# Recurrence and maxout MLP on one core: fixed issue order, short first blocks, most inputs transposed by DMA through DRAM, four tokens per partition in the stores

## The chip, the cores and the metric

The kernel runs on one core of a Trainium2 chip. The metric is device time in microseconds (us), as the median of a few executions. "Span" is the time from the first to the last instruction in one profiled execution; it is about 2 us shorter than the time of the same execution. TensorE is PE in the profile (PEld its weight loads), VectorE is DVE, ScalarE is ACT, GpSimd is POOL, SyncE is SP.

## The reference

```python
# x, f_logit: (4, 6144, 256); lower_bound: (256,); w1, w2: (256, 1024); w_out: (1024, 256); float32
f = lb + (1 - lb) * sigmoid(f_logit)
h = f[:, t] * h + (1 - f[:, t]) * x[:, t]        # for every t; y[:, t] = h
g = maximum(y @ w1, y @ w2)
out = g @ w_out                                  # (24576, 256)
```

Both kernels use max(y w1, y w2) = relu(y (w2 - w1)) + y w1. So the first layer needs one product with wd, the scaled difference of w2 and w1, and the second layer sums y (w1 w_out), whose matrix w13 is computed once, and relu(...) w_out. The features lie on the 128 partitions, because the recurrence is a scan along the tokens of each feature. f and x lie in memory with tokens as rows, so they have to be transposed.

## The kernel before

Tokens go in blocks of TB = 512. Inputs come in chunks of 1,024 tokens by a GpSimd DMA that casts to BF16, and TensorE transposes them in 128x128 pieces:

```python
def turn(j, slot):                       # 2 of the 16 transposes of a block
    c, o = home[j]
    s, q = divmod(slot, FC // 2)
    if q == 0:
        turned[j, s] = ps_t.tile([P, KC, TB], BF16, name=("fT", "xT")[s])
    dst = turned[j, s]
    for h in range(KC):
        nc.tensor.transpose(dst[:, h, q * P : (q + 1) * P],
            ins[c][s][:, o * NSB + q, h * P : (h + 1) * P], ident_b[:])
# [...]
# project(): the second layer; 128 consecutive tokens are the stationary tile
tok = slice(i * P, (i + 1) * P)
steps = [(y[:, kc, tok], w13[:, kc, :]) for kc in range(KC)]
steps += [(rts[j, fc][:, tok], wob[:, fc, :]) for fc in range(FC)]
# [...] stores of 256 tokens, rows of 1 KB
nc.sync.dma_start(out=out[r0 : r0 + 2 * P, :].rearrange("(r p) d -> p r d", p=P), in_=osb[:])
# [...] main loop: only TensorE's order is set by hand
with tc.manual_schedule(engines={ENG.PE}):
    for j in range(NBLK + 1):
        # [...] load(c) four blocks ahead
        for fc in range(FC):
            if j < NBLK: hidden(j, fc)            # first layer, 2 matmuls of 512 columns, relu on ACT
            if j > 0: project(j - 1, fc)          # 5 matmuls of 256 columns
            if j + 2 < NBLK: turn(j + 2, fc)      # 2 transposes
        if j + 2 < NBLK: recurrence(j + 2)        # sigmoid on ACT; v, ff and two scans on DVE
```

One pass of the inner loop is called a slot below; eight slots are a block.

Of the kernel before, what the change touches and what calls it, by code (L numbers as in the profile page):

```python
# [8 lines left out]
FP32 = mybir.dt.float32  # L9
# [4 lines left out]
P = 128  # L14
# [3 lines left out]
def kernel(  # L18
# [18 lines left out]
    NSB = TB // P  # L37
    CH = 2 * TB
    assert S % CH == 0
    NBB = S // TB  # L40
    NBLK = B * NBB
    chunks = [(0, 1), (1, 1)] + [(j, 2) for j in range(2, NBLK, 2)]
    home = {j + o: (c, o) for c, (j, n) in enumerate(chunks) for o in range(n)}
# [3 lines left out]
    inpool = ctx.enter_context(tc.tile_pool(name="inp", bufs=4))  # L47
# [5 lines left out]
        tc.tile_pool(name="ps_t", bufs=1, space=bass.MemoryType.PSUM)  # L53
# [7 lines left out]

    ident_f = const.tile([P, P], FP32)
    make_identity(nc, ident_f[:])
    ident_b = const.tile([P, P], BF16)
    nc.vector.tensor_copy(out=ident_b[:], in_=ident_f[:])  # L65

    om = const.tile([P, KC], FP32)
    nom = const.tile([P, KC], FP32)
    lbc = const.tile([P, KC], FP32)
    nc.sync.dma_start(out=lbc[:], in_=lower_bound.rearrange("(h p) -> p h", p=P))  # L70
# [5 lines left out]
    ins = {}  # L76

    def load(c):
        j, n = chunks[c]
        b, k = divmod(j, NBB)  # L80
        t0, nt = k * TB, n * TB
        ni = nt // P
        tiles = []
        for name, src in (("fn", f_logit), ("xn", x)):
            nat = inpool.tile([P, CH // P, D], BF16, name=name)
            nc.gpsimd.dma_start(  # L86
                out=nat[:, 0:ni, :],
                in_=src[b, t0 : t0 + nt, :].rearrange("(i p) d -> p i d", p=P),
            )
            tiles.append(nat)  # L90
        ins[c] = tiles

    ys = {}
    turned = {}

    def turn(j, slot):
        c, o = home[j]
        s, q = divmod(slot, FC // 2)
        if q == 0:
            turned[j, s] = ps_t.tile([P, KC, TB], BF16, name=("fT", "xT")[s])  # L100
        dst = turned[j, s]
        for h in range(KC):
            nc.tensor.transpose(  # L103
                dst[:, h, q * P : (q + 1) * P],
                ins[c][s][:, o * NSB + q, h * P : (h + 1) * P],
                ident_b[:],
            )

    def recurrence(j):
        fT, xT = turned[j, 0], turned[j, 1]  # L110
        prev = ys.get(j - 1) if j % NBB else None
        u = midpool.tile([P, KC, TB], BF16, name="u")
        nc.scalar.activation(out=u[:], in_=fT[:], func=AF.Sigmoid, scale=-1.0)  # L113
        v = midpool.tile([P, KC, TB], BF16, name="v")
        nc.vector.tensor_tensor(out=v[:], in0=u[:], in1=xT[:], op=ALU.mult)  # L115
        ff = midpool.tile([P, KC, TB], BF16, name="ff")
        y = ypool.tile([P, KC, TB], BF16, name="y")
        for h in range(KC):
            nc.vector.tensor_scalar(  # L119
                out=ff[:, h, :],  # L120
                in0=u[:, h, :],
                scalar1=nom[:, h : h + 1],
                scalar2=1.0,
                op0=ALU.mult,
                op1=ALU.add,
            )
            nc.vector.tensor_tensor_scan(  # L127
                out=y[:, h, :],
                data0=ff[:, h, :],
                data1=v[:, h, :],  # L130
                initial=0.0 if prev is None else prev[:, h, TB - 1 : TB],
                op0=ALU.mult,
                op1=ALU.add,
            )
        ys[j] = y

    def weight_prep():
        w1n = wpool.tile([P, KC, DFF], FP32)
        w2n = wpool.tile([P, KC, DFF], FP32)
        wob = wpool.tile([P, FC, D], BF16)  # L140
        w1b = wpool.tile([P, KC, DFF], BF16)
        wdf = wpool.tile([P, KC, DFF], FP32)
        wd = wpool.tile([P, KC, DFF], BF16)
        for g in range(2):
            cols = slice(g * DFF // 2, (g + 1) * DFF // 2)
            for w, src in ((w1n, moe_w1), (w2n, moe_w2)):
                nc.scalar.dma_start(
                    out=w[:, :, cols],
                    in_=src[:, cols].rearrange("(kc p) f -> p kc f", p=P),
                )  # L150
        nc.gpsimd.dma_start(
            out=wob[:], in_=moe_w_out.rearrange("(fc p) c -> p fc c", p=P)
        )
        for g in range(2):
            cols = slice(g * DFF // 2, (g + 1) * DFF // 2)
            nc.scalar.copy(out=w1b[:, :, cols], in_=w1n[:, :, cols])  # L156
            nc.vector.tensor_tensor(  # L157
                out=wdf[:, :, cols],
                in0=w2n[:, :, cols],
                in1=w1n[:, :, cols],  # L160
                op=ALU.subtract,
            )
            for kc in range(KC):
                nc.vector.tensor_scalar_mul(
                    out=wd[:, kc, cols], in0=wdf[:, kc, cols], scalar1=om[:, kc : kc + 1]
                )
        w1T = wpool.tile([P, FC, D], BF16)
        for kc in range(KC):
            for g in range(FC // 4):
                pt = ps_d.tile([P, TB], BF16, name="dT")  # L170
                for q in range(4):
                    fc = 4 * g + q
                    nc.tensor.transpose(
                        pt[:, q * P : (q + 1) * P],
                        w1b[:, kc, fc * P : (fc + 1) * P],
                        ident_b[:],
                    )
                nc.scalar.copy(
                    out=w1T[:, 4 * g : 4 * g + 4, kc * P : (kc + 1) * P],
                    in_=pt[:].rearrange("p (q d) -> p q d", q=4),  # L180
                )
        w13 = wpool.tile([P, KC, D], BF16)
        for kc in range(KC):
            psw = ps_o.tile([P, 2, D], FP32, name="psO")
            for fc in range(FC):
                nc.tensor.matmul(  # L186
                    psw[:, 0, :],
                    lhsT=w1T[:, fc, kc * P : (kc + 1) * P],
                    rhs=wob[:, fc, :],
                    start=(fc == 0),  # L190
                    stop=(fc == FC - 1),
                )
            nc.scalar.mul(w13[:, kc, :], psw[:, 0, :], om[:, kc : kc + 1])
        return wd, wob, w13
# [3 lines left out]
    def hidden(j, fc):  # L198
        y = ys[j]
        dT = ps_d.tile([P, TB], FP32, name="dT")  # L200
        for kc in range(KC):
            nc.tensor.matmul(  # L202
                dT[:],
                lhsT=wd[:, kc, fc * P : (fc + 1) * P],
                rhs=y[:, kc, :],
                start=(kc == 0),
                stop=(kc == KC - 1),
            )
        rt = rpool.tile([P, TB], BF16, name="rt")
        nc.scalar.activation(out=rt[:], in_=dT[:], func=AF.Relu)  # L210
        rts[j, fc] = rt

    pos = {}

    def project(j, slot):
        i, half = divmod(slot, 2)
        g, r = divmod(i, 2)
        y = ys[j]
        if r == 0 and half == 0:
            pos[j] = ps_o.tile([P, 2, D], FP32, name="psO")  # L220
        ps = pos[j]
        tok = slice(i * P, (i + 1) * P)
        steps = [(y[:, kc, tok], w13[:, kc, :]) for kc in range(KC)]
        steps += [(rts[j, fc][:, tok], wob[:, fc, :]) for fc in range(FC)]
        n = len(steps)
        for s in range(half * n // 2, (half + 1) * n // 2):
            nc.tensor.matmul(  # L227
                ps[:, r, :],
                lhsT=steps[s][0],
                rhs=steps[s][1],  # L230
                start=(r == 0 and s == 0),
                stop=(r == 1 and s == n - 1),
                skip_group_check=True,
            )
        if r == 1 and half == 1:
            osb = opool.tile([P, 2, D], FP32, name="osb")
            nc.vector.tensor_copy(out=osb[:], in_=ps[:])  # L237
            r0 = j * TB + 2 * g * P
            nc.sync.dma_start(
                out=out[r0 : r0 + 2 * P, :].rearrange("(r p) d -> p r d", p=P),  # L240
                in_=osb[:],
            )

    started = {c: chunks[c][0] for c in range(len(chunks))}
    ahead = 4
    for c in range(len(chunks)):
        if started[c] < ahead:
            load(c)
    for slot in range(FC):
        turn(0, slot)  # L250
    recurrence(0)
    wd, wob, w13 = weight_prep()
    for slot in range(FC):
        turn(1, slot)
    recurrence(1)
    with tc.manual_schedule(engines={ENG.PE}):
        for j in range(NBLK + 1):
            for c in range(len(chunks)):
                if started[c] == j + ahead:
                    load(c)  # L260
            for fc in range(FC):
                if j < NBLK:
                    hidden(j, fc)
                if j > 0:
# [35 lines left out]
```

## Time and profile before

| | before |
|---|---|
| time, median | 445.1 us |
| span of the profiled execution | 443.3 us |
| TensorE busy | 423.0 us, 95% |
| slot with transposes / without | 1.09 us / 0.98 us |
| main loop runs freely from | 25.2 us |
| last matmul ends to end of span | 4 us |

From the page of the kernel before: busy time and instructions of each engine; then two DMA queues (packets, megabytes, share of the time of 16 DMA engines; q0 is GpSimd's, q1 that of SP); then the chain that ended last, by engine.

```profile
PE 423.0 (95%) x3488; PEld 309.8 (70%) x3488; DVE 247.0 (56%) x345; ACT 278.5 (63%) x442; POOL 44.9 (10%) x57
...
q0 software_dynamic: 50992, 25.69, 46.1%
q1 hardware_dynamic: 26384, 25.17, 18.4%
...
PE 94%; DMA 4%; POOL 1%; DVE 0%; issue 0%; POOLq 0%
```

TensorE binds. What a transpose costs it is read from the timeline (start in us, duration, engine, line, instruction, count), in the steady part and in the last block, where nothing is left to transpose.

```profile
206.59 0.28 PE L103 MATMUL xT<-ident_b,xn 128*128 128x128 bf16 x2
206.71 0.59 PE L202 MATMUL dT<-y,wd 128*128 128x512 bf16 x2
207.14 0.71 PE L227 MATMUL psO<-wob,rt 128*128 128x256 bf16 x5
207.68 0.28 PE L103 MATMUL xT<-ident_b,xn 128*128 128x128 bf16 x2
...
428.87 0.59 PE L202 MATMUL dT<-y,wd 128*128 128x512 bf16 x2
429.30 0.38 PE L227 MATMUL psO<-w_182,y 128*128 128x256 bf16 x2
429.52 0.49 PE L227 MATMUL psO<-wob,rt 128*128 128x256 bf16 x3
429.85 0.59 PE L202 MATMUL dT<-y,wd 128*128 128x512 bf16 x2
```

Matmuls overlap, so starts are to be compared, not durations. The two transposes start at 206.59 us and the next matmul at 206.71: about 0.06 us each. The slot is 207.68 - 206.59 = 1.09 us, and 429.85 - 428.87 = 0.98 us without transposes, so by the slots a transpose costs 0.11 / 2 = 0.055 us. All 768 of them are 768 x 0.055 = 42 us.

The start, in the timeline of TensorE (in brackets the idle time before and what ended it):

```profile
13.38 1.01 PE L103 MATMUL fT<-ident_b,fn 128*128 128x128 bf16 x8 [13.38 <-DVE ident_b L65]
...
18.02 0.39 PE L202 MATMUL dT<-y,wd 128*128 128x512 bf16 x1 [0.34 <-DVE y L127]
...
23.51 1.91 PE L186 MATMUL psO<-wob,w1T 128*128 128x256 bf16 x16 [1.83 <-DMA wob<-in_moe_w_out_dram]
```

### The profile page before, as it was taken

Reading aid. Unit: us, or ns where it says so; the run is one execution under the profiler, and the core shown is the slowest. Engines: PE = TensorE matmul, PEld = TensorE weight load, DVE = VectorE, ACT = ScalarE, POOL = GpSimd, SP = SyncE. Lnnn points to the kernel's source line nnn. Section 1 sums busy time; section 2 is a strip of 40 time slices with the busy share of each in tenths; the row PEclk is TensorE's granted clock in tenths of the full one; section 3 lists DMA queues with packets and bytes.
Section 4 is the critical chain, followed back from the end, with each engine's and each line's share of the span. In section 5 each row is a group of like instructions: output and inputs, shape, how many; then the busy total and the mean of one; then the engine's idle time right before and its main releaser. Section 6 shows DMA issues by size and latency. Waiting matters only on the chain.

```text
span 443.3 us, 8434 instructions
## 1 busy us (share of the span) xinstructions
PE 423.0 (95%) x3488; PEld 309.8 (70%) x3488; DVE 247.0 (56%) x345; ACT 278.5 (63%) x442; POOL 44.9 (10%) x57
## 2 busy tenths in 40 slices
PE   0689999999999999999999999999999999999996
PEld 0567777777777777777777777777777777777765
DVE  2744665565556546655655565466546655654631
ACT  3666666666666766666666666666766666666661
POOL 6300101001001001010010010010100100000000
PEclk9999999999999999999999999999999999999999
DMA  8999769487487495694874965956948731212112
GB/s 221 198 198 215 138 124 152 83 146 123 94 140 127 91 163 94 123 151 87 146 119 99 140 121 96 163 95 124 149 85 149 120 95 48 72 49 71 57 64 95
DMA packets 78501, 53.49 MB, mean 121 GB/s; under 512 B 2688, under 2 KB 77440, under 8 KB 78464
## 3 DMA queue, kind: packets, MB, share of 16 engines
q0 software_dynamic: 50992, 25.69, 46.1%
q1 hardware_dynamic: 26384, 25.17, 18.4%
q10 hardware_dynamic: 1088, 2.10, 1.5%
q8 instruction: 27, 0.44, 0.4%
q14 instruction: 10, 0.08, 0.1%
HBM read 53.48 MB, written 25.17 MB: 177 GB/s over the span
## 4 chain that ended last, share of the span: by engine, by line
PE 94%; DMA 4%; POOL 1%; DVE 0%; issue 0%; POOLq 0%
PE psO L227 47%; PE dT L202 37%; PE xT L103 5%; PE fT L103 5%; DMA wob<-in_moe_w_out_dram 4%; POOL fn L86 1%; POOL xn L86 1%; PE psO L186 0%; DVE osb L237 0%; POOL ident_f masks.py:199 0%; POOL ident_f masks.py:197 0%; POOLq masks.py:199 0%; POOLq L284 0%
## 5 line engine op out<-in xcount | busy, mean ns | idle before, releaser
L210 ACT ACTIVATE rt<-dT 128x512 bf16<-128x512 f32 x384 | 226.8, 597 | 142.2 <-PE dT L202 142.1
L227 PE MATMUL psO<-wob,rt 128*128 128x256 bf16 x1536 | 229.8, 273 | 0.0
L202 PE MATMUL dT<-y,wd 128*128 128x512 bf16 x768 | 228.2, 379 | 1.1 <-DVE y L127 1.1
L227 PEld LDWEIGHTS <-rt 128*128 128x128 bf16 x1536 | 150.3, 98 | 57.5
L237 DVE COPY osb<-psO 128x512 f32<-128x512 f32 x96 | 66.4, 692 | 152.5 <-PE psO L227 152.5
L127 DVE TENSOR_TENSOR_SCAN y<-ff,y,v 128x512 bf16<-128x512 bf16 x88 | 108.2, 1272 | 1.5
L227 PE MATMUL psO<-w_182,y 128*128 128x256 bf16 x384 | 73.3, 273 | 0.0
L227 PEld LDWEIGHTS <-y 128*128 128x128 bf16 x384 | 37.6, 98 | 44.4
L103 PE MATMUL fT<-ident_b,fn 128*128 128x128 bf16 x384 | 52.2, 221 | 13.4 <-DVE ident_b L65 13.4
L202 PEld LDWEIGHTS <-wd 128*128 128x128 bf16 x768 | 59.6, 98 | 0.9 <-DVE y L127 0.5
L103 PE MATMUL xT<-ident_b,xn 128*128 128x128 bf16 x384 | 52.2, 221 | 0.0
L113 ACT ACTIVATE u<-fT 128x1024 bf16<-128x1024 bf16 x48 | 49.1, 1024 | 4.9 <-PE fT L103 2.3
L103 PEld LDWEIGHTS <-fn 128*128 128x128 bf16 x384 | 37.3, 99 | 19.2 <-DMA fn<-in_f_logit_dram 11.0
L86 POOL DMA_DIRECT2D fn<-in_f_logit_dram x25 | 21.9, 874 | 237.0 <-PE fT L103 174.2
L119 DVE TENSOR_SCALAR ff<-u,nom 128x512 bf16<-128x512 bf16 x96 | 29.9, 354 | 25.6 <-ACT u L113 25.6
L103 PEld LDWEIGHTS <-xn 128*128 128x128 bf16 x384 | 37.4, 99 | 4.8
L115 DVE TENSOR_TENSOR v<-u,xT 128x1024 bf16<-128x1024 bf16 x48 | 32.5, 677 | 3.9 <-PE xT L103 3.9
L86 POOL DMA_DIRECT2D xn<-in_x_dram x25 | 21.6, 866 | 68.2 <-PE dT L202 64.9
L127 DVE TENSOR_TENSOR_SCAN y<-ff,v 128x512 bf16<-128x512 bf16 x8 | 9.4, 1211 | 0.1
L157 DVE TENSOR_TENSOR wdf<-w2n,w1n 128x1024 f32<-128x1024 f32 x2 | 2.5, 1226 | 6.5 <-DMA w2n<-in_moe_w_dram 6.5
L156 ACT CAST w1b<-w1n 128x1024 bf16<-128x1024 f32 x2 | 2.1, 1045 | 4.6 <-DMA w1n<-in_moe_w_dram 4.6
L186 PE MATMUL psO<-wob,w1T 128*128 128x256 bf16 x16 | 1.9, 272 | 1.8 <-DMA wob<-in_moe_w_out_dram 1.8
(18 smaller groups left out, 15.2 us busy)
## 6 DMA issues: line engine op xcount, KB each, us to landing
out_dram<-osb SPq DMA_DIRECT2D x96, 256.0 KB, 2.7
fn<-in_f_logit_dram POOLq DMA_DIRECT2D x23, 512.0 KB, 8.2
xn<-in_x_dram POOLq DMA_DIRECT2D x23, 512.0 KB, 8.4
w1n<-in_moe_w_dram ACTq DMA_DIRECT2D x2, 512.0 KB, 6.2
w2n<-in_moe_w_dram ACTq DMA_DIRECT2D x2, 512.0 KB, 7.4
fn<-in_f_logit_dram POOLq DMA_DIRECT2D x2, 256.0 KB, 10.3
xn<-in_x_dram POOLq DMA_DIRECT2D x2, 256.0 KB, 10.9
wob<-in_moe_w_out_dram POOLq DMA_DIRECT2D x1, 512.0 KB, 17.0
```

The source lines that it names most:

```text
L86: nc.gpsimd.dma_start(out=nat[:, 0:ni, :], in_=src[b, t0 : t0 + nt, :].rearrange("(i p) d -> p i d", p=P),)
L103: nc.tensor.transpose(dst[:, h, q * P : (q + 1) * P], ins[c][s][:, o * NSB + q, h * P : (h + 1) * P], ident_b[:],)
L113: nc.scalar.activation(out=u[:], in_=fT[:], func=AF.Sigmoid, scale=-1.0)
L115: nc.vector.tensor_tensor(out=v[:], in0=u[:], in1=xT[:], op=ALU.mult)
L119: nc.vector.tensor_scalar(out=ff[:, h, :], in0=u[:, h, :], scalar1=nom[:, h : h + 1], scalar2=1.0, op0=ALU.mult, op1=ALU.add,)
L127: nc.vector.tensor_tensor_scan(out=y[:, h, :], data0=ff[:, h, :], data1=v[:, h, :], initial=0.0 if prev is None else prev[:, h, TB - 1 : T ...
L156: nc.scalar.copy(out=w1b[:, :, cols], in_=w1n[:, :, cols])
L157: nc.vector.tensor_tensor(out=wdf[:, :, cols], in0=w2n[:, :, cols], in1=w1n[:, :, cols], op=ALU.subtract,)
L202: nc.tensor.matmul(dT[:], lhsT=wd[:, kc, fc * P : (fc + 1) * P], rhs=y[:, kc, :], start=(kc == 0), stop=(kc == KC - 1),)
L210: nc.scalar.activation(out=rt[:], in_=dT[:], func=AF.Relu)
L227: nc.tensor.matmul(ps[:, r, :], lhsT=steps[s][0], rhs=steps[s][1], start=(r == 0 and s == 0), stop=(r == 1 and s == n - 1), skip_group_che ...
L237: nc.vector.tensor_copy(out=osb[:], in_=ps[:])
```

## The change

It means to take most transposes off TensorE, to start earlier, and to store in longer runs. All engines get a fixed issue order. Of 26 chunks, f of 21 and x of 16 are cast into a DRAM scratch and loaded back by a transposing DMA; the rest, the first five chunks among it, stay on TensorE (176 transposes). The first blocks have 256 tokens, the weights come in four pieces of 256 columns, and an output tile takes every fourth token, so that each partition stores four consecutive rows, 4 KB.

```diff
+        sizes = [256, 256, 512] if b == 0 else []
+        sizes += [CH] * ((S - sum(sizes)) // CH)
 ...
+    def by_xbar(c, s):
+        return c >= 5 and (s == 0 or c % 4 != 3)
 ...
+    NSCR = 6
+    scratch = [[dram.tile([CH, D], BF16, name=f"scr{s}_{q}") for q in range(NSCR)] for s in range(2)]
 ...
+            elif by_xbar(c, s):                                # fetch(c)
+                scr = scratch[s][uses[s] % NSCR]
+                uses[s] += 1
+                nc.gpsimd.dma_start(
+                    out=scr[0:nt, :].rearrange("(p i) d -> p (i d)", p=P),
+                    in_=src.rearrange("(p i) d -> p (i d)", p=P))
 ...
+    def cross(c):
+        for s in range(2):
+            if by_xbar(c, s):
+                dst = inpool.tile([P, KC, CH], BF16, name=("fT", "xT")[s])
+                nc.sync.dma_start_transpose(out=dst[:, :, 0:nt], in_=held[c, s][0:nt, :])
 ...
+            left = y[:, s, i:nb:ns] if s < KC else rts[j, s - KC][:, i:nb:ns]
 ...
+                        out=out[r0 : r0 + nb, :].rearrange("(p n) d -> p n d", p=P),
 ...
+    LEAD_FETCH = 10       # fetch() is recorded 10 blocks ahead, cross() 5
+    LEAD_CROSS = 5
+    with tc.manual_schedule():
+        fetch(0)
+        fetch(1)
+        for g in range(NG):
+            fetch_w(g)                 # w2 and w1, columns 256 g .. 256 g + 255, on SP
+        nc.gpsimd.dma_start(out=wob[:], ...)
+        fetch(2)
 ...           # weight preparation interleaved with blocks 0 to 2
+        for j in range(1, NBLK + 1):
+            ahead("fetch", fetch, j + LEAD_FETCH)
+            ahead("cross", cross, j + LEAD_CROSS)
 ...           # the slots; gate() is the sigmoid of block j + 2, scan_steps() of j + 1
```

## The prediction

> **What bounds the kernel now.** TensorE. The page gives it 423.0 of 443.3 us busy (95%), and the chain that ended last is 94% TensorE. VectorE (56%), ScalarE (63%) and the DMA engines have room. In the steady timeline one slot (2 transposes, 2 matmuls of 512 columns, 5 of 256) takes 1.09 us, a block of 512 tokens 8.71 us; the last block, without transposes, runs slots of 0.98 us, 7.84 us a block. A transpose thus costs 0.055 us of TensorE time in the pipeline, although the table of groups shows 221 ns each; 768 are about 42 us. About 376 us is the two layers. The other 22 us: no matmul before 13.4 us, holes until 25 us (the second-layer weights landed at 23.5 us; that wait is in the chain), 4 us after the last matmul.
>
> **What the change does.**
> - f of 21 of 26 chunks and x of 16 go by DMA: 176 input transposes stay on TensorE, 592 leave: -32 us.
> - The start: blocks of 256 tokens, weights in four pieces, second-layer weights ahead of chunk 2. First-layer work should start near 9 us instead of 18. But what must land before the loop runs freely (weights 2.5 MB, chunks 0 to 3 4 MB of source) is the 6.5 MB that took 23.5 us before. I expect chunk 3 near then, and 2 to 4 us of waiting for it. Net gain at the start about 5 us.
> - The last block copies and stores each 128 tokens by itself: -1 us.
> - Added on TensorE: warm-up and FP32 transposes, early, where it idles anyway.
> - VectorE (about 5.3 us a block) and ScalarE (5.8) stay within 7.84 us.
> - Stationary tiles of every fourth token: the weight load is 98 ns behind a matmul of about 108 ns. I assume that the step costs nothing; the Trainium skill, TensorE: Matmul & The Clock Gate, Weight-path perf modes, allows fast weight load for such steps. No trace here shows it yet.
>
> **DMA, the risk.** Loads take 46.1% of 16 engines now, stores 18.4% (DMA queue table). The change writes 19.4 MB of BF16 to DRAM and reads it back transposed, in 37 transfers of 0.5 MB. The Trainium skill, DMA: Bandwidth & Descriptors, Latency and other measured facts, gives 261 GB/s for one transposing case: an estimated 2.0 us each, 18% of the new span; this trace shows none. Longer runs of loads and stores should shrink their shares. The sum stays below 100%. If a transposing transfer took over about 4 us of all 16 engines, DMA would bind.
>
> **Sum.** TensorE work about 421 - 32 = 389 us, idle 22 down to about 16, some scattered waits: span about 406, plus the 1.8 us between span and time: **408 us**, 8 in 10 between 400 and 420. Faster by over 2% 0.95, within 2% 0.03, slower 0.02.
>
> **What would show it.** Steady slots of 0.98 us (1.03 where x is still transposed); 176 input transposes; no wait of the sigmoid for a transposing DMA after about 60 us; first-layer matmuls from about 9 us, a wait for chunk 3 near 20 us; DMA share below 90% later.
>
> **What would make it wrong.** Slow transposing DMAs, so that the sigmoid waits for fT or VectorE for xT (420 us and more); stores stuck behind transposes in the SP queue, holding output buffers; strided weight loads above 108 ns, stretching all 1,920 second-layer matmuls; VectorE's new order, scans after output copies, delaying y.

## The result, and the profile after

The time fell from 445.1 us to 418.3 us (four runs, 418.2 to 421.4). The ratio is 0.942, with a 95% interval of 0.937 to 0.946. Ratios are the mean time of one kernel's fast runs over that of the other's in the same rounds, so they are not quite the ratio of the medians. Executions over 1.5% slower than the fastest of the same kernel are left out of the means. The result is correct.

The same lines of the page after:

```profile
PE 395.5 (95%) x2872; PEld 304.8 (73%) x2920; DVE 239.3 (58%) x354; ACT 274.1 (66%) x457; POOL 30.9 (7%) x57
...
q1 hardware_dynamic: 87152, 46.93, 49.4%
q0 software_dynamic: 13184, 25.43, 37.6%
...
PE 83%; DMA 15%; issue 1%; ACT 0%; POOL 0%; DVE 0%; POOLq 0%; ACTq 0%
```

TensorE still binds over most of the span, but 15% of the chain is now DMA, all of it before 64 us. The steady slot is what was predicted, 201.79 - 200.82 = 0.97 us:

```profile
200.82 0.59 PE L301 MATMUL dT<-y,wd 128*128 128x512 bf16 x2
201.25 0.71 PE L330 MATMUL psO<-wob,rt 128*128 128x256 bf16 x5
201.79 0.59 PE L301 MATMUL dT<-y,wd 128*128 128x512 bf16 x2
```

Two things differ from the prediction. First, the start. Below are ScalarE's scalings of the four weight pieces, each waiting for its piece, then TensorE's first matmul of the first layer and the first of the main loop.

```profile
10.05 0.91 ACT L251 ACTIVATE w1s<-w1n,om 128x256 f32<-128x256 f32 x2 [4.18 <-DMA w1n<-in_moe_w_dram]
...
11.13 1.22 PE L301 MATMUL dT<-y,wd 128*128 128x256 bf16 x4 [4.00 <-DVE wd L257]
...
13.18 0.91 ACT L251 ACTIVATE w1s<-w1n,om 128x256 f32<-128x256 f32 x2 [2.23 <-DMA w1n<-in_moe_w_dram]
...
16.27 0.91 ACT L251 ACTIVATE w1s<-w1n,om 128x256 f32<-128x256 f32 x2 [0.37 <-DMA w1n<-in_moe_w_dram]
...
19.35 0.91 ACT L251 ACTIVATE w1s<-w1n,om 128x256 f32<-128x256 f32 x2 [0.28 <-DMA w1n<-in_moe_w_dram]
...
25.82 0.38 PE L301 MATMUL dT<-y,wd 128*128 128x256 bf16 x2
```

A piece lands every 3.1 us, and the loop begins at 25.8 us. The old loop ran freely from 25.2 us and had then done 10 first-layer matmuls of 512 columns; the new one has done 16 of 256. So the new start is no further along: the 97th of the 1,920 second-layer matmuls ends at 50.3 us, against 48.5 us before. From 20 to 25 us the granted TensorE clock averaged 0.66 here (1.00 in the old kernel from 20 to 30 us), which slowed the preparation too; no run separates this from the late weights.

Second, TensorE stands still at 62.9 us. SP issues the first two transposing DMAs, the sigmoid waits for the first, and TensorE waits for ScalarE (timeline):

```profile
33.33 10.61 SPq L122 DMA_TRANSPOSE fT<-scr_0_90  x1
44.04 19.65 SPq L122 DMA_TRANSPOSE xT<-scr_0_96  x1
...
64.12 1.06 ACT L160 ACTIVATE u<-fT 128x1024 bf16<-128x1024 bf16 x1 [4.02 <-DMA fT<-scr_0_90]
...
65.71 1.01 PE L301 MATMUL dT<-y,wd 128*128 128x512 bf16 x2 [2.83 <-ACT rt L309]
```

The transfer of 0.5 MB is issued at 33.3 us and lands after 30.7 us. The granted TensorE clock is 0.50 from 65.1 to 68.5 us, behind the wait, so the wait costs a little more than it lasts. What the DMA queues moved between 50 and 60 us (packets, MB, share of 16 engines) says why:

```profile
DMA packets 260, 2.16 MB, mean 216 GB/s; under 512 B 193, under 2 KB 193, under 8 KB 193
...
q0 software_dynamic: 128, 2.10, 97.7%
q1 hardware_dynamic: 129, 0.03, 2.0%
```

GpSimd's queue moved 128 packets and SP's 129: one for one. But only 64 of the 128 carry data, 2.10 MB / 64 = 32.8 KB each and 2.4 us long in the trace; the other 64 have 4 B. (They are in the first line: under 512 B are 129 + 64 = 193.) The packets of the transposing DMA have 256 B, so the transpose got about one byte in 65. The Trainium skill (DMA: Bandwidth & Descriptors, Queues, rings and completion order) says that each DMA engine takes turns between queues at packet granularity; the counts agree.

### The profile page after: what moved, and what is told of

It is laid out like the page before. It is cut to its first block, busy times and chain, and to the rows that moved or that the text cites. A ratio compares the mean times of both kernels' runs of the same rounds, so it can differ in the third digit from the quotient of the medians.

```text
span 415.8 us, 7247 instructions
## 1 busy us (share of the span) xinstructions
PE 395.5 (95%) x2872; PEld 304.8 (73%) x2920; DVE 239.3 (58%) x354; ACT 274.1 (66%) x457; POOL 30.9 (7%) x57
## 3 DMA queue, kind: packets, MB, share of 16 engines
q1 hardware_dynamic: 87152, 46.93, 49.4%
## 4 chain that ended last, share of the span: by engine, by line
PE 83%; DMA 15%; issue 1%; ACT 0%; POOL 0%; DVE 0%; POOLq 0%; ACTq 0%
PE psO L330 48%; PE dT L301 34%; DMA fT<-scr_0_90 7%; DMA scr_0_90<-in_f_logit_dram 6%; DMA xn<-in_x_dram 2%; PE tT L151 1%; ACT u L160 0%; POOL fn L111 0%; ACT rt L309 0%; DVE osb L339 0%; POOL ident_f masks.py:199 0%; POOL ident_f masks.py:197 0%; POOLq masks.py:199 0%; ACTq L160 0%; POOLq L439 0%
## 5 line engine op out<-in xcount | busy, mean ns | idle before, releaser
L309 ACT ACTIVATE rt<-dT 128x512 bf16<-128x512 f32 (+1 forms) x392 | 225.7, 587 | 117.8 <-PE dT L301 115.7
L301 PE MATMUL dT<-y,wd 128*128 128x512 bf16 (+1 forms) x736 | 221.6, 378 | 10.1 <-DVE wd L257 7.0
L330 PEld LDWEIGHTS <-rt 128*128 128x128 bf16 x1536 | 169.6, 113 | 42.9 <-issue 0.6
L194 DVE TENSOR_TENSOR_SCAN y<-ff,y,v 128x512 bf16<-128x512 bf16 (+1 forms) x90 | 109.2, 1255 | 0.0
L301 PEld LDWEIGHTS <-wd 128*128 128x128 bf16 x784 | 71.9, 98 | 16.9 <-DVE wd L257 9.5
L174 DVE TENSOR_SCALAR ff<-u,nom 128x512 bf16<-128x512 bf16 (+1 forms) x98 | 29.7, 347 | 0.0
L151 PE MATMUL tT<-ident,xn 128*128 128x128 bf16 x124 | 23.6, 228 | 0.0
L184 DVE TENSOR_TENSOR v<-u,tT 128x1024 bf16<-128x1024 bf16 (+1 forms) x17 | 11.3, 664 | 7.6 <-PE tT L151 4.0
L151 PEld LDWEIGHTS <-xn 128*128 128x128 bf16 x124 | 12.3, 103 | 0.3
L111 POOL DMA_DIRECT2D xn<-in_x_dram x9 | 7.9, 883 | 2.3 <-DMA xn<-in_x_dram 2.2
```

The source lines that it names most:

```text
L111: nc.gpsimd.dma_start(out=nat[:, 0 : nt // P, :], in_=src.rearrange("(i p) d -> p i d", p=P),)
L151: nc.tensor.transpose(dst, src, ident[:] if src.dtype == BF16 else ident_f[:])
L174: nc.vector.tensor_scalar(out=ff[:, h, 0:nb], in0=u[:, h, 0:nb], scalar1=nom[:, h : h + 1], scalar2=1.0, op0=ALU.mult, op1=ALU.add,)
L184: nc.vector.tensor_tensor(out=v[:, :, 0:nb], in0=u[:, :, 0:nb], in1=turned[j, 1], op=ALU.mult)
L194: nc.vector.tensor_tensor_scan(out=y[:, h, 0:nb], data0=ff[:, h, 0:nb], data1=v[:, h, 0:nb], initial=init, op0=ALU.mult, op1=ALU.add,)
L301: nc.tensor.matmul(dT[:, 0:nb], lhsT=wd[:, kc, fc * P : (fc + 1) * P], rhs=y[:, kc, 0:nb], start=(kc == 0), stop=(kc == KC - 1),)
```

## The experiments

Each edit is to the changed kernel ("after"), unless it says otherwise. Twelve kernels were run. Theories: A, the gain is all in the transposes, the start gave nothing, and the wait near 62 us comes from loads that GpSimd queues ahead of the transposes. B, the rival of each run, is told in its expectation; in the later runs A too is what the expectation calls so.

### All transposes back on TensorE

```diff
-        return c >= 5 and (s == 0 or c % 4 != 3)
+        return False
```

> All transposes back on TensorE; issue order, short first blocks, weight pieces and 4 KB stores stay as in the changed kernel. Theory A (the whole gain is the 592 transposes that left TensorE; the new start gained almost nothing because at 25.8 us it has done no more work than the old one at 25.2 us): time = 418.3 + 592 x 0.0545 - about 3.5 (the wait near 62 us goes) = about 447 us, within 1% of the kernel before. Rival B (the start and the stores gained the 5 to 6 us that the prediction gave them, and the transposes gained less): about 439 us.

444.87 us, ratio to before 0.999 (0.997 to 1.000): the same as the kernel before. Fixed order, short blocks, weights in pieces and long stores together gained nothing measurable. Rival B falls. (The profiled execution of this run was the slowest of its four, 447.8 us; its loop began at 27.4 us.)

### Three scratch buffers in place of six

```diff
-    NSCR = 6
+    NSCR = 3
```

> Three DRAM scratch buffers per input in place of six, so GpSimd cannot queue as many loads ahead. Theory A (the first transposing DMA, 30.7 us from issue to landing, is starved by the loads that GpSimd queued ahead of need): it lands in under 20 us, before 55 us, the TensorE wait near 62 us goes, time about 415 us. Rival B (the DMA engines are short in total): landing of later chunks slips, the wait moves to later blocks, time 418 us or more.

413.03 us, ratio 0.929 (0.927 to 0.930), below the interval of the changed kernel (0.937 to 0.946). GpSimd, with fewer buffers, first stops issuing loads after 26.2 us instead of 41.3. The first transpose lands in 17.0 us instead of 30.7, no sigmoid waits for a transpose, and TensorE has no gap from 30 us to the end. Between 42 and 51 us the queues of this run moved:

```profile
DMA packets 4145, 1.33 MB, mean 148 GB/s; under 512 B 3172, under 2 KB 4129, under 8 KB 4144
...
q1 hardware_dynamic: 3168, 0.83, 83.0%
q0 software_dynamic: 976, 0.49, 61.4%
```

With the long loads done, SP's queue gets 3,168 packets through in 9 us. The landing times in the traces say the same of every run: in all ten correct runs with transposing DMAs, the changed kernel included, the first one landed 0.8 to 2.6 us after the last of the loads that GpSimd had issued ahead, and that load landed anywhere from 42.8 to 66.7 us (49.6 and 50.7 us here, 63.1 and 64.0 us in the changed kernel). From this run and the first, which both have the new start and no wait for a transpose, the worth of 592 transposes is 444.87 - 413.03 = 31.8 us.

Late in this run a transpose runs beside nothing else (353 to 355 us):

```profile
DMA packets 1850, 0.48 MB, mean 241 GB/s; under 512 B 1849, under 2 KB 1849, under 8 KB 1849
...
q1 hardware_dynamic: 1849, 0.47, 132.6%
```

The share over 100% for one queue alone shows that these shares sum packet times that overlap or reach out of the window; they are no measure of how full the engines are. 0.47 MB in 2 us, about 235 GB/s, is close to the 261 GB/s that the prediction took from the Trainium skill (DMA: Bandwidth & Descriptors, Latency and other measured facts). The size of a transpose was right; that it keeps this speed in company was the silent assumption.

### Loads held back until the weights are in

```diff
+    hold = const.tile([P, 1], FP32)
 ...
+        nc.gpsimd.tensor_copy(out=hold[:], in_=w1n[:, KC - 1, DFF - 1 : DFF])
         fetch(2)
```

> GpSimd reads one column of the last weight piece before it issues chunk 2 and all later loads, so the weights share the DMA engines with little. Both theories: last weight piece near 13 us instead of 19.4, first loop near 19 to 20 us instead of 25.8. Theory A (the gain at the start is given back, because chunk 3 and then the first transposed chunk come when the DMA engines have moved what lies before them): wait for chunk 3 near 22 to 25 us, longer TensorE wait before the first transposed block (7 us or more in place of 3), time 417 to 419 us. Rival B (the weights alone hold the start): about 412 us.

422.86 us, ratio 0.952 (0.949 to 0.955): slower than the changed kernel by about 1%. The profiled execution was the slowest of its six (427.7 us), so its waits may be longer than those of the others. The last weights landed at 16.3 us, not at 13, and the loop began at 24.4 us, not at 19 to 20. The gain of 1.4 us there was lost at once and more: TensorE waited for chunk 3 (0.6 and 0.8 us in its timeline), and the sigmoid waited twice for a transpose, as ScalarE's timeline shows.

```profile
67.65 1.06 ACT L160 ACTIVATE u<-fT 128x1024 bf16<-128x1024 bf16 x1 [7.27 <-DMA fT<-scr]
...
184.45 1.06 ACT L160 ACTIVATE u<-fT 128x1024 bf16<-128x1024 bf16 x1 [4.85 <-DMA fT<-scr]
```

Rival B (the weights alone hold the start) falls. The direction of theory A holds, but its sizes were off, and the second wait was not foreseen.

### Held loads and three scratch buffers

> Both edits: held loads and three scratch buffers. If the two waits hide each other (theory A): the gain is larger than the sum of the two single gains, time 410 to 413 us. If the DMA engines are short in total at the start (rival B): no better than three scratch buffers alone, about 415 us or more.

414.78 us, ratio 0.932 (0.931 to 0.934), no better than three buffers alone. The two gains do not add. The chain of waits of this run shows why: with the weights early, chunk 3 is late. Its x, issued at 18.4 us, landed at 28.8 us.

```profile
18.44 10.34 DMA xn<-in_x_dram
```

### Tokens in a row, stores of 1 KB rows

```diff
-            left = y[:, s, i:nb:ns] if s < KC else rts[j, s - KC][:, i:nb:ns]
+            tok = slice(i * P, (i + 1) * P)
+            left = y[:, s, tok] if s < KC else rts[j, s - KC][:, tok]
 ...
-  .rearrange("(p n) d -> p n d", p=P)
+  .rearrange("(n p) d -> p n d", p=P)
```

> The changed kernel with six scratch buffers, but each output tile takes 128 tokens in a row, stored in 1 KB rows as before; only the four tokens per partition are undone. Theory A (stationary tiles of every fourth token cost nothing, because the weight load, 113 ns in place of 98, stays hidden, and the long store rows save DMA time that only the wait near 62 us can feel): the steady slot stays 0.98 us, weight loads fall to 98 ns, time 418 to 421 us. Rival B (the stride stretches the second layer): slots get shorter and the time falls below 416 us.

421.34 us, ratio 0.945 (0.942 to 0.949). This interval overlaps that of the changed kernel, so the time difference is not clear. The weight loads of the second layer, in the groups of the changed kernel and then of this run (last numbers: busy us, mean ns | idle before, and what ended most of it):

```profile
L330 PEld LDWEIGHTS <-rt 128*128 128x128 bf16 x1536 | 169.6, 113 | 42.9 <-issue 0.6
```

```profile
L331 PEld LDWEIGHTS <-rt 128*128 128x128 bf16 x1536 | 150.7, 98 | 58.6 <-issue 0.6
```

The step of four tokens costs 15 ns per weight load and nothing in time: this run's slots are also 0.98 us. Rival B falls. The short stores brought 105,072 packets on SP's queue in place of 87,152, and the sigmoid waited a second time here (3.0 us, at 115 us), which suits the idea that long stores help when the DMA engines are crowded, but one profile does not prove it.

### All of x by the transposing DMA

```diff
-        return c >= 5 and (s == 0 or c % 4 != 3)
+        return c >= 5
```

With three scratch buffers:

> All of x from chunk 5 on goes through the transposing DMA, with three scratch buffers. 80 transposes leave TensorE: -4.4 us. Theory A (the DMA engines, at about 85% of the span, have room for five more transposing transfers of about 3.5 us of all engines each): about 409 us. Rival B (with them the DMA engines are short, three quarters of x was the balance): waits for fT or xT appear, 413 us or more.

With six:

> The changed kernel with its six scratch buffers, and all of x from chunk 5 on through the transposing DMA. With three buffers this took 440 us. Theory A (the DMA engines themselves are short: two transposes, two loads and two stores per chunk took 17.2 us between 170 and 350 us, TensorE needs 15.7): 430 to 450 us again, the sigmoid waiting for fT. Rival B (three buffers were too shallow for it): about 414 us, as 80 fewer transposes on TensorE promise.

440.49 us with three buffers (ratio 0.992, 0.988 to 0.996), and 453.21 us with six. In the second, two of four runs counted as slow; its two fast runs were 445.6 and 450.6 us (ratio 1.007, 1.000 to 1.014). So with five more transposing transfers 0.8% of gain over the kernel before is left, or none. From the waits and the queues of the run with three buffers:

```profile
POOL scr L104 <- DMA fT<-scr: 283.1, 18, 23.7
...
ACT u L160 <- DMA fT<-scr: 31.6, 10, 7.3
...
DVE v L184 <- DMA xT<-scr: 6.4, 5, 1.9
```

```profile
q1 hardware_dynamic: 97552, 49.56, 67.9%
q0 software_dynamic: 8144, 25.43, 35.3%
```

The sigmoid waits ten times, 31.6 us in total, and the shares of the two queues sum to over 100%. In the chain of waits, a chunk takes 17.4 us between 265 and 352 us (five chunks in 86.8 us); TensorE needs 15.6 us (two blocks of 7.82). Depth was not the reason, since six buffers were slower still. That there was room for all of x (theory A of the first run) was wrong. That the DMA engines are short (theory A of the second) fits, but is not shown: they moved 182 GB/s in this stretch, and 227 GB/s in the changed kernel from 120 to 160 us, and the sum of the shares proves nothing (see the 132.6% above). SP's one queue is a rival. In its timeline it issues without a pause, transposes and stores one behind the other:

```profile
265.12 9.83 SPq L122 DMA_TRANSPOSE fT<-scr  x1
275.04 6.00 SPq L122 DMA_TRANSPOSE xT<-scr  x1
281.14 1.01 SPq L353 DMA_DIRECT2D out_dram<-osb  x2
282.25 4.07 SPq L122 DMA_TRANSPOSE fT<-scr  x1
```

No run separates the two. Three quarters of x could go this way and all of it could not; nothing between was tried.

### Wide weight pieces, and chunk 3 in halves

```diff
-        for g in range(NG):
+        for g in range(0, NG, 2):          # and fetch_w takes 512 columns
             fetch_w(g)
```

```diff
-        sizes = [256, 256, 512] if b == 0 else []
+        sizes = [256, 256, 512, 512, 512] if b == 0 else []
 ...
-        return c >= 5 and (s == 0 or c % 4 != 3)
+        return c >= 6 and (s == 0 or c % 4 != 3)
```

Both with three scratch buffers; the first edit alone, then both:

> Weights in two pieces of 512 columns (2 KB rows) in place of four of 256 (1 KB rows), three scratch buffers. Theory A (the short rows made the weights slow: the old kernel had all of them at 12 us): last weights at 13 to 15 us in place of 19, main loop from 22 to 23 us in place of 26.5, then bound by chunk 3, time 410 to 412 us. Rival B (only the share of the loads beside them slows the weights): unchanged, 413 us.

> As the run with wide weight pieces, and chunk 3 loaded as two chunks of 512 tokens, so that its first half lands about 4 us earlier. If chunk 3 binds once the weights come earlier (theory A): main loop runs freely 3 to 4 us earlier than in the run with wide pieces alone if weights were early there, time 407 to 410 us. If the weights bind (rival B): no gain over 413 us.

Wide pieces alone: 412.24 us, ratio 0.926 (0.924 to 0.928), an interval that overlaps that of three buffers alone. ScalarE no longer waited for the second half of the weights, yet the loop still began at 25.8 us: the chain of waits then ran through VectorE's scans of block 1, the weight preparation and TensorE's work behind it. Theory A had the direction for the weights (the last landed at 16.4 us, against 19.5 with four pieces; 13 to 15 was expected) and was wrong on the gain.

Both edits: 414.87 us, ratio 0.929 (0.925 to 0.934), with runs from 411.3 to 419.7 us. The loop began at 24.1 us, and a 3.3 us wait of the sigmoid near 60 us was back. Between 50 and 58 us the queues moved:

```profile
q1 hardware_dynamic: 315, 0.08, 104.7%
q0 software_dynamic: 10, 0.13, 7.7%
```

SP's transposes had only 315 packets through in 8 us, beside only 10 load packets, so one-for-one turns do not explain these 8 us. But the loads were not done: the last landed at 59.4 us, and the first transpose at 61.6. (The expectation of the run with two buffers, below, takes the loads for done by about 40 us, which is wrong.) In the trace the transposes moved in bursts: packets that took up to 3.4 us ended together at 53.3, 55.7 and 58.2 us, each time about 0.2 us after load packets of 32.8 KB had ended (53.1, 55.5 and 58.0 us). So a few long load packets seem to have held up all the transposes. The trace does not name the DMA engine of a packet, so how they did it is not shown.

### Two scratch buffers: two wrong results, and one that is right

> Two scratch buffers per input in place of six, nothing else changed. Theory A (the first transposing DMA suffers under the loads that GpSimd queues ahead): it lands no later than with three buffers (51 us), no wait near 62 us, time 412 to 414 us if depth two still covers the steady part. Rival B (two buffers are too shallow): new waits for fT later, time over 416 us.

> Wide weight pieces, chunk 3 in two halves, two scratch buffers. With three buffers the main loop began near 24.3 us, 2 us earlier than with chunk 3 whole, and lost it again in a 3.3 us wait for the first transposed chunk. Theory A (less queued ahead removes that wait): 409 to 411 us. Rival B (that wait is not from loads queued ahead, as the loads were done by about 40 us there and the transposes still crept until 61 us): wait stays, 413 to 416 us.

Both gave wrong results (relative errors of 0.64 and 0.67), which was not intended. Loads are recorded ten blocks ahead and transposes five, so up to three chunks lie between them. With two buffers the third load is recorded before the transpose that should read the first, and overwrites it, in the kernel's own order. Three buffers are enough, and those runs were correct. The times (414.64 and 411.45 us) belong to programs with other dependencies, and no theory is read from them. The second was mended:

```diff
     NSCR = 2
-    LEAD_FETCH = 10
+    LEAD_FETCH = 8
```

> The run before gave a wrong result: with two scratch buffers and loads recorded ten blocks ahead, a buffer was written again, in the kernel's own order, before the transposing DMA that should read it; no theory can be read from it. Here loads are recorded eight blocks ahead, so that every transpose stands before the load that reuses its buffer; wide weight pieces and the halves of chunk 3 stay. Theory A (the 3.3 us wait of the three-buffer run comes from what GpSimd queued ahead): first transposed chunk lands before 55 us, no wait near 60 us, time 409 to 412 us. Rival B (that wait has another cause): it stays, 413 to 416 us.

412.10 us, ratio 0.927 (0.925 to 0.928), correct. The first transpose landed in 12.7 us, against 28.3 us with three buffers, and no sigmoid waited for one. Less queued ahead removed the wait, as theory A says. The time is that of wide pieces with three buffers. So the fastest correct versions are three scratch buffers (413.0 us, one constant), or with wide pieces 412.1 to 412.2 us.

## Why the prediction was right or wrong, point by point

The prediction named 408 us with a range of 400 to 420; the measured 418.3 us lies inside, near the upper end. The main mechanism was right and two terms of the sum were mis-sized.

- "592 leave: -32 us". Right. 176 input transposes are left in the profile (124 and 44 in BF16, 8 in FP32), the slot is 0.98 us, and the runs put the worth at 31.8 us.
- "Net gain at the start about 5 us". Wrong, and the largest error. The run with all transposes on TensorE had every other part of the change and took 444.87 us, so the gain was 0. The prediction expected first-layer work from 9 us; it came at 11.1 us, then once for each weight piece, the last at 20.4 us. It also expected chunk 3 to be the wait, and no wait for it appears. Holding the loads moved the limit to chunk 3, and wide weight pieces moved it to the fixed order of the preparation: three limits lie close together, and removing one gains little. The prediction itself said that the same 6.5 MB have to arrive, and yet counted 5 us.
- "some scattered waits". Too small. There was one wait for the first transposed chunk, near 62 us. With three buffers the last matmuls came 3.7 us earlier, although that loop began 0.6 us later, so the wait and the slow clock behind it cost about 4.3 us.
- "The last block copies and stores each 128 tokens by itself: -1 us". The tail went from 4.0 to 3.5 us.
- The sum: 406 us of span were predicted, and 415.8 measured. The run with three buffers, which has no such wait, has 412.2. So about 6 us of the miss are the start and the tail, 3.7 us net the wait. The rest of the 10 us is the gap between span and time (2.4 us, not 1.8).
- "Stationary tiles of every fourth token ... the step costs nothing". Right: loads of 113 ns, above the 108 ns that the prediction feared, and yet the slot did not grow. The Trainium skill (TensorE: Matmul & The Clock Gate, Weight-path perf modes) allows fast weight load for such steps; the profile shows that the cost is small.
- DMA, "an estimated 2.0 us each", "the sum stays below 100%". The size is right for a transpose alone (0.47 MB in 2 us), and the shares sum to 87%. But that is a mean over the span: the share was 1.18 from 120 to 160 us and 0.48 from 300 to 350 us, so "DMA share below 90% later" did not hold. By its packets' times, waiting included, a transposing transfer took 3.3 us of 16 engines between 120 and 300 us, and 5.1 us in the run with all of x and three buffers (265 to 352 us); the prediction's own limit of about 4 us lies between. And shares say nothing of who waits: beside loads with packets of 32.8 KB a transpose with packets of 256 B took 30.7 us to land. The prediction had named slow transposes as what could make it wrong; it had not seen that the loads queued beside them would be the reason, nor how near the limit the kernel was.
- What stays open: how a few load packets could hold the transposes to 315 packets in 8 us in the run with chunk 3 in halves; whether the DMA engines or SP's one queue are short when all of x goes by DMA; and whether shorter packets of the scratch loads would cure the wait as fewer buffers do. The packet counts argue for it, but no run tried it.

## What to carry to other kernels

Before counting on a DMA that is cheap by itself, ask what is queued beside it and how long the other queue's packets are: less prefetch was faster here. Test a bundle of changes by undoing its largest part alone; here one line showed that the start, which looks much better in the code, gained nothing. Where a buffer is reused between two stages recorded at different leads, count the buffers that the order itself needs.

## What the Trainium skill lacked or had wrong

- DMA: Bandwidth & Descriptors, Queues, rings and completion order: turns by packet are stated, and the counts agree (128 and 129 packets in 10 us). What that does to a transposing DMA is not: its packets are 256 B (0.47 MB in 1,849), so it got 0.03 MB while the loads got 2.10 MB.
- The same page, SWDGE vs HWDGE vs iDMA, gives packets of at most 4,096 B as the preferred size. The cast from DRAM to DRAM with long runs shows 32.8 KB per data packet in the trace (2.10 MB in 64). Whether a packet of the trace is what the page calls a packet is not shown.
- The same page, Latency and other measured facts: 261 GB/s for a transpose is near what one that runs alone shows (0.47 MB in 2 us, about 235 GB/s). Nothing is said of it in company: in the changed kernel the f transposes took from 4.9 to 30.7 us to land for 0.5 MB each.
- TensorE: Matmul & The Clock Gate, PE-mode transpose: about 275 ns for a 128x128 transpose in a kernel. The groups here show 221 ns, but between neighbours in the stream one costs 0.055 us, which is what its removal gained.
- TensorE: Matmul & The Clock Gate, Weight-path perf modes: the range of steps is stated, the cost is not. A step of four elements took 113 ns in place of 98, hidden behind the matmuls.
